# Loading the r and k tiles without their padding rows, seven loads in flight, and a newly drawn order

## The chip, the cores and the metric

The kernel runs on one core of a Trainium2 chip. The metric is the device time of one execution in microseconds; the median of several executions is compared.

## The reference

Two stages follow each other. The first is a linear attention with a decaying state, for 4 batches, 8 heads, 768 tokens and 48 dimensions a head:

```
cur   = (u * k_t) outer v_t
y_t   = r_t @ (state + cur)
state = w * state + k_t outer v_t
```

The second is a gated block on x, which is y with its heads laid side by side (384 columns):

```
h = relu(x @ w_in);  u, v = halves of h            (512 columns each)
v_n = (v - mean) / sqrt(var + 1e-6)
v_s = w_spatial @ v_n + b_spatial                  (over the 768 tokens)
out = (u * v_s) @ w_out
```

## The kernel before

**Chunks.** The 768 tokens of a batch are cut into 6 chunks of 128, 24 chunks for the 4 batches. For each chunk four transfers are issued in `load_chunk`: `rk` (r and k with the dimensions on the rows, for the scores), `rs` and `ks` (r and k with the tokens on the rows) and `rkv` (v). The `rk` tile has 128 rows of 4 KB: two heads share a tile, one on rows 0 to 63 and one on rows 64 to 127, and of each 64 rows 48 hold data. The other 16 are zeros, which the host writes and every load brings along. There are two buffers for `rk` tiles. `prep` multiplies the tile in place with powers of the decay (`tt`), for the first 13 chunks as two instructions that may go to POOL (GpSimd) or DVE (VectorE), then as one on DVE. Since the powers of the padding rows are 1, their zeros stay zeros. `scores` reads the tile on TensorE (PE), `apply` reads its r half (in the first eight chunks straight from the tile, later from a copy in tile `A`).

**The gated block.** `moe_v`, `moe_u`, `moe_sp` and `moe_out` follow once their chunks are there. Every float32 product is made of three matmuls of a high and a low part (`mm3`). The weights w_in and w_out arrive as 64-bit numbers and are split into high and low parts on DVE, ACT (ScalarE) and PE in the first part of the kernel (`convert_in`, `convert_out`), those of w_spatial by `split`.

**The order.** No engine's order is written by hand. The class `Plan` collects tasks with their costs on each engine, their buffers and what they depend on, and walks through them in simulated time, so that each engine's instructions come out in one order. All inputs go through the queue of SP (SyncE). The planner has a model of that queue: `landing` says when a load lands, from a delay to the first byte (`TO_BYTE`), a lower rate in the first microseconds (`SLOW`) and a rate after (`RATE`). `LANES` is the number of loads that may be in flight: every load waits, on the chip too, until the load six places before it has landed. `Fetch` models the fetching of PE's instructions and `Clock` TensorE's clock. Before the walk, `shake` goes through the list `SEEDS`; each seed stands for a small random change of some tasks' due times and of their leanings to one engine. With another list of seeds the whole order is another.

Of the kernel before, what the change touches and what calls it, by code (L numbers as in the profile page):

```python
# [8 lines left out]
F32 = mybir.dt.float32  # L9
# [3 lines left out]
ALU = mybir.AluOpType  # L13
AX = mybir.AxisListType

B, H, S, D = 4, 8, 768, 48
# [3 lines left out]
P = 128  # L20
C = 128
# [3 lines left out]
NP = H // 2  # L25
# [14 lines left out]
LEAN = 4.0  # L40
AHEAD = 0.3
ALONE = 1000.0
CALM, LATE = 80.0, dict(DVE=1.0, SP=1.0)
SEEDS = (786675, 590737, 650567, 473966, 410529, 555426, 907183, 123843, 647820, 960324, 828658, 912501, 134089,
         159232, 4393, 523669, 612611, 964576, 241432, 346394, 906374, 371707, 92393, 507276, 798277, 338735, 176835,
         444512, 896537, 239246, 993420, 861971, 866320, 990367, 131959, 191835, 802215, 648123, 562279, 390339,
         978361, 670519, 812235, 451845, 697243, 382570,)
BIAS = dict(DVE=3.0, ACT=3.5)
MOST_IN, MOST_OUT = 2, 1

# [3 lines left out]
CHAIN = dict(PE=0.0, DVE=0.115, ACT=0.11, POOL=0.0, SP=0.0)  # L54
SWITCH = {"bs": 0.095, "br": 0.095, "by": 0.095, "sb": 0.215, "sy": 0.11, "rb": 0.105, "yb": 0.105}
STAY = 1.0
LANES = 6
PORT = dict(DVE=(0.07, 0.0, 0.0), POOL=(0.15, 0.06, 0.02))


# [58 lines left out]
class Plan:  # L119
# [1 line left out]

    SLOW, PART = 210e3, (6.0, 42.0)
    RATE, TO_BYTE, BEHIND_BYTE = (395e3, 395e3, 262e3), (2.2, 2.9, 1.3), (0.5, 0.5, 0.4)

    def __init__(self, slots, wait):
        self.wait, self.sent = wait, []
# [45 lines left out]
    def shake(self):  # L174
        for seed in SEEDS:
            rnd = random.Random(seed)
            share, size = rnd.choice((0.01, 0.03, 0.1, 0.3)), rnd.choice((1.0, 3.0, 8.0))
            width, at = rnd.choice((3.0, 12.0, 50.0, 1000.0)), rnd.uniform(-10.0, 330.0)
            for t in self.tasks:
                if abs(t.due - at) < width and rnd.random() < share:  # L180
                    t.due += rnd.uniform(-size, size)
                    for w in t.ways:
                        w.lean += rnd.uniform(-size, size)
# [20 lines left out]
    def landing(self, line, at, nbytes):  # L204
        part = sum(at > x for x in self.PART)
        line = max(line, at + self.TO_BYTE[part])
        slow = min(nbytes / self.SLOW, max(0.0, 5.2 - line))
        line += slow + (nbytes - slow * self.SLOW) / self.RATE[part]
        return line, line + self.BEHIND_BYTE[part]

# [2 lines left out]
    def lane(self, at, landed):  # L213
        return max(at, landed[-LANES]) if len(landed) >= LANES else at

    def run(self):
# [8 lines left out]
        while ready:  # L225
# [71 lines left out]
            if way.nbytes:  # L297
                self.sent.append(made.ins)
                if len(self.sent) > LANES:
                    self.wait(made.ins, self.sent[-1 - LANES].name)  # L300
        assert all(t.end is not None for t in self.tasks)
# [3 lines left out]
def fused_kernel(ctx, tc, rkT, rkvE, rkvL, wT, uB, w_in, w_sp, b_sp, w_out, out):  # L305
# [9 lines left out]
    SLOTS = dict(rk=2, rs=2, ks=2, rkv=3, a=1, A=2, t=4, X=2, gt=4, u=8, vs=2, g=3, ob=2, pm=5, ps=1, xp=1, x=2, s=2, t1=1, dg=2, q=2)  # L315
    SLOTS |= {f"w{x}{n}": 1 for x in "ab" for n in range(NS)}
    const = ctx.enter_context(tc.tile_pool(name="const", bufs=1))
# [7 lines left out]
    plan = Plan(SLOTS, wait)  # L325
    T = {}

    def tile_of(key, shape, dtype=F32):
        key = key[:2]
        if key not in T:  # L330
            home = psum if key[0] in ("pm", "ps", "xp") else sbuf
            T[key] = home.tile(shape, dtype, name=key[0], tag=f"{key[0]}{plan.slot[key]}")
        return T[key]
# [6 lines left out]
    def dve(n, f, r, w, cost=None, two=False, due=None):  # L340
        plan.add([("DVE", n / 960 + 0.07 if cost is None else cost, f, two)], r, w).most = due
# [7 lines left out]
    def pair(n, f, r, w, ways="DVE POOL", lean=0.0):  # L349

        engine = dict(DVE=nc.vector, POOL=nc.gpsimd)
        cost = dict(DVE=n / 960 + 0.07, POOL=n / 480 + 0.17)
        plan.add([(e, cost[e], lambda e=e: engine[e].tensor_tensor(**f()), True, 0, lean if e == "DVE" else 0.0)  # L353
                  for e in ways.split()], r, w)
# [12 lines left out]
    def load(key, shape, dtype, src, nbytes, view=None, due=None):  # L367
        def f():
            t = tile_of(key, shape, dtype)
            return nc.sync.dma_start(out=view(t) if view else t, in_=src)  # L370
        plan.add([("SP", 0.45, f, False, nbytes)], (), [key], lag=0).most = due


    wt = const.tile([P, NP], F32, name="wt")
    ub = const.tile([P, DM], F32, name="ub")
    tt = const.tile([P, NP, C], F32, name="tt")
# [14 lines left out]
    def eye():  # L391
        return tile_of(EYE, [P, P])

    def neg(n=1):
        return tile_of(NEG, [P, 2, P], F32R)[:, n]
# [65 lines left out]
    TTP = ("pm", "tt")  # L461
    TN = [("c", "tn", 0), ("c", "tn", 1)]

    def load_chunk(m):
        b, c = divmod(m, NC)
        load(("rk", m), [P, 2, NP, C], F32, rkT[b, c], P * 2 * NP * C * 4)
        n, src = (ROW_E, rkvE[m]) if m < EC else (ROW, rkvL[m - EC])
        load(("rs", m), [P, DM], F32, src[:, 0:DM], P * DM * 4)
        load(("ks", m), [P, DM], F32, src[:, OK:OV], P * DM * 4)
        load(("rkv", m), [P, ROW - OV], F32, src[:, OV:n], P * (n - OV) * 4, lambda t: t[:, 0:n - OV])  # L470
# [116 lines left out]
    def prep(m):  # L587
        RK, RS, KS, DG, A = ("rk", m), ("rs", m), ("ks", m), ("dg", m), ("a", m)
        a = lambda: tile_of(A, [P, 2, 2, 2, HC])
        r_, k_, kn, rn = (RK + ("r",), RK + ("k",), KS + ("kn",), RS + ("rn",))  # L590
        rk = lambda: T[RK]
        TT = [("c", "t0"), ("c", "t1"), ("c", "t2")]
        if m < EARLY:
            for i, key in ((1, k_), (0, r_)):
                plan.add([("POOL", 1.24, lambda i=i: nc.gpsimd.tensor_tensor(
                    out=rk()[:, i], in0=rk()[:, i], in1=tt, op=ALU.mult), True),
                    ("DVE", 0.6, lambda i=i: nc.vector.tensor_tensor(
                        out=rk()[:, i], in0=rk()[:, i], in1=T[TTP].rearrange("p (n c) -> p n c", n=NP),
                        op=ALU.mult), False, 0, LEAN if i else -9.0)], [RK, TTP, *TT], [key])
        else:  # L600
            dve(1024, lambda: nc.vector.tensor_tensor(out=rk(), in0=rk(), in1=tt.unsqueeze(1).to_broadcast(  # L601
                [P, 2, NP, C]), op=ALU.mult), [RK, *TT], [r_, k_], cost=1.14, two=True)
        n_, k0 = (lambda: T[RS]), (lambda: T[KS])
        lean = ALONE if m < QUIET else LEAN
        pair(DM, lambda: dict(out=n_(), in0=n_(), in1=k0(), op=ALU.mult), [RS, KS], [rn], lean=lean)
        pair(DM, lambda: dict(out=n_(), in0=n_(), in1=ub, op=ALU.mult), [rn, ("c", "ub")], [rn], lean=lean)
        dve(DM - 8, lambda: nc.vector.tensor_reduce(out=tile_of(DG, [P, H]), in_=n_().rearrange("s (h d) -> s h d", h=H),
                                                axis=AX.X, op=ALU.add), [rn], [DG])
        pair(DM, lambda: dict(out=k0(), in0=k0(), in1=tn_f, op=ALU.mult), [KS, rn, *TN], [kn], lean=lean)
        pair(432, lambda: dict(  # L610
            out=a().rearrange("s b q z t -> s (b q z) t"), in0=diag.unsqueeze(1).to_broadcast([P, H, HC]),
            in1=T[DG].unsqueeze(2).to_broadcast([P, H, HC]), op=ALU.mult), [DG, ("c", "diag")], [A], lean=lean)
        if m >= EC:
            move(RK + ("r",), ("A", m), "r", [(64 * (1 - t), t, slice(2 * b, 2 * b + 2), 64 * (t ^ b))
                                              for b in range(2) for t in range(2)],
                 lambda p, h: rk()[h:h + 64, 0, p])

    def move(src, dst, part, places, source):

        for o, t, p, h in places:  # L620
            n = (p.stop - p.start) * C
            out = lambda o=o, t=t, p=p: tile_of(dst, [P, 2, NP, C])[o:o + 64, t, p]
            plan.add([("SP", 0.45, lambda out=out, p=p, h=h: nc.sync.dma_start(out=out(), in_=source(p, h)), False, 64 * n * 4),
                      ("ACT", (n + 250) / 1200, lambda out=out, p=p, h=h: nc.scalar.copy(out(), source(p, h))),  # L624
                      ("DVE", n / 1920 + 0.15, lambda out=out, p=p, h=h: nc.vector.tensor_copy(out=out(), in_=source(p, h)),  # L625
                       True, 0, LEAN)],
                     [src], [dst + ((part, t, p.start),)])
# [411 lines left out]
    for i in range(NM):  # L1039
        n = FIRST[i] if i < NC else len(steps) if i == NM - 1 else int(10 + (i - 5) * per / 6)  # L1040
# [20 lines left out]
    for b in range(B):  # L1061
        for c in range(NC):
            m = b * NC + c
# [93 lines left out]
```

## Time and profile before

| | |
|---|---|
| median of 3 runs | 326.91 us (326.5 to 327.86) |
| profiled execution | 327.6 us, of which the span of the profile is 325.9 us |
| TensorE (PE) busy | 309.7 us, 95% of the span |
| DVE, ACT, POOL busy | 245.4, 198.6, 250.9 us |
| mean granted TensorE clock | 0.995 |
| DMA | 49.14 MB, mean 151 GB/s |

The span runs from the first to the last instruction; the profiled execution has 1.7 us more around it. An engine's busy time counts the time in which at least one of its instructions ran. The granted clock is a share of TensorE's full speed. The DMA share is the mean busy share of the core's 16 DMA engines, and it can come out a little over 1.

### The profile page before, as it was taken

To read this page: it belongs to the slowest core of one execution; us is meant where nothing else is said; L and a number is where in the kernel's file an instruction comes from. 1 tells how busy PE (TensorE), PEld (TensorE's weight loads), DVE (VectorE), ACT (ScalarE), POOL (GpSimd) and SP (SyncE) were. 2 spreads that over 40 slices of the span, in tenths; PEclk is the share of its full clock that TensorE was granted. 3 is DMA by queue.
4 is the path that set the end of the run, shared out by engine and by line. 5 is a ranking of instruction groups with operands and counts; after the bars stand their busy time and mean duration, and the time that the engine had idled before them with its cause. 6 is when DMAs were issued, how large, how long until landed. Compare 5 with 4: busy or idle time off the path is not lost.

```text
span 325.9 us, 10933 instructions
## 1 busy us (share of the span) xinstructions
PE 309.7 (95%) x4574; PEld 283.3 (87%) x4574; DVE 245.4 (75%) x465; ACT 198.6 (61%) x492; POOL 250.9 (77%) x235
## 2 busy tenths in 40 slices
PE   2787999999999999999999999999999999999995
PEld 1466788999999888998979998999988989999995
DVE  6899986799962899858999996489998431727830
ACT  4346984847643887767759477686576663433422
POOL 3878999999988999899999875688999440358700
PEclk9997999999999999999999999999999999999999
DMA  6999768685255836154346245264140010010013
GB/s 229 377 393 382 257 219 278 217 295 181 91 172 185 270 100 235 32 178 141 106 166 203 51 177 171 81 205 139 51 147 5 25 50 2 0 51 24 0 42 105
DMA packets 21233, 49.14 MB, mean 151 GB/s; under 512 B 2496, under 2 KB 12096, under 8 KB 21184
## 3 DMA queue, kind: packets, MB, share of 16 engines
q1 hardware_dynamic: 21040, 48.34, 43.2%
q8 instruction: 36, 0.59, 0.8%
q14 instruction: 13, 0.11, 0.1%
q10 hardware_dynamic: 144, 0.10, 0.1%
HBM read 43.58 MB, written 4.72 MB: 148 GB/s over the span
## 4 chain that ended last, share of the span: by engine, by line
PE 68%; DVE 10%; POOL 8%; DMA 7%; ACT 3%; issue 2%; SPq 0%; POOLq 0%; ACTq 0%; DVEq 0%
PE pm L762 20%; PE pm L764 19%; PE pm L763 19%; PE xp L719 5%; DMA rs<-rkvE 4%; PE ps L638 3%; POOL rs L353 2%; DMA rk<-rkT 2%; DMA wb<-w_sp 2%; PE ps L657 1%; DVE rk L601 1%; POOL wb L353 1%; DVE A L625 1%; POOL t L353 1%; DVE a L353 1%
## 5 line engine op out<-in xcount | busy, mean ns | idle before, releaser
L762 PE MATMUL pm<-wa,t 128*128 128x384 f32 x120 | 41.3, 344 | 0.0
L763 PE MATMUL pm<-wa,t 128*128 128x384 f32 x120 | 40.5, 337 | 0.0
L764 PE MATMUL pm<-wa,t 128*128 128x384 f32 x120 | 40.4, 336 | 0.0
L353 POOL TENSOR_TENSOR t<-vs,t 128x384 fp32r<-128x384 f32 x26 | 32.6, 1269 | 1.4 <-ACT t L358 1.4
L762 PE MATMUL pm<-x,wi_h 128*128 128x384 f32 x93 | 32.0, 344 | 0.0
L764 PE MATMUL pm<-x,wi_l 128*128 128x384 f32 x93 | 31.2, 336 | 0.0
L763 PE MATMUL pm<-x,wi_h 128*128 128x384 f32 x93 | 31.2, 336 | 0.0
L624 ACT COPY A<-rk 64x256 f32<-64x256 f32 x54 | 21.8, 404 | 15.1 <-PE xp L719 5.3
L353 POOL TENSOR_TENSOR rs<-rs,ks 128x384 f32<-128x384 f32 x21 | 26.8, 1276 | 4.4 <-DMA ks<-rkvL 2.9
L762 PE MATMUL pm<-wi_h,x 128*128 128x512 f32 x69 | 28.5, 413 | 0.3 <-DVE g L933 0.3
L762 PE MATMUL pm<-wo_h,gt 128*128 128x384 f32 x84 | 28.6, 340 | 0.0
L764 PE MATMUL pm<-wo_h,gt 128*128 128x384 f32 x84 | 28.3, 336 | 0.0
L763 PE MATMUL pm<-wo_l,gt 128*128 128x384 f32 x84 | 28.3, 336 | 0.0
L764 PE MATMUL pm<-wi_h,x 128*128 128x512 f32 x69 | 27.7, 401 | 0.0
L763 PE MATMUL pm<-wi_l,x 128*128 128x512 f32 x69 | 27.5, 399 | 0.0
L353 POOL TENSOR_TENSOR ks<-ks,tn 128x384 f32<-128x384 f32 x23 | 25.1, 1092 | 0.0
L353 POOL TENSOR_TENSOR rs<-rs,ub 128x384 f32<-128x384 f32 x22 | 23.4, 1062 | 1.3
L353 POOL TENSOR_TENSOR X<-vs,X 128x384 f32<-128x384 f32 x9 | 10.6, 1175 | 17.6 <-ACT vs L844 17.2
L933 DVE TENSOR_TENSOR g<-pm,bb 128x384 f32<-128x384 f32 x32 | 17.5, 549 | 8.6 <-PE pm L764 8.2
L353 POOL TENSOR_TENSOR a<-diag,dg 128x512 f32<-128x512 f32 x16 | 17.2, 1077 | 8.5 <-ACT A L624 7.6
L353 POOL TENSOR_TENSOR gt<-u,gt 128x384 fp32r<-128x384 f32 x20 | 22.6, 1142 | 1.3 <-ACT gt L358 1.3
L762 PEld LDWEIGHTS pm<-wa,t 128*128 128x128 f32 x120 | 22.6, 188 | 1.1 <-DVE g L933 0.6
(182 smaller groups left out, 960.4 us busy)
## 6 DMA issues: line engine op xcount, KB each, us to landing
rk<-rkT SPq DMA_DIRECT2D x24, 512.0 KB, 5.6
rkv<-rkvL SPq DMA_DIRECT2D x16, 512.0 KB, 3.8
out<-ob SPq DMA_DIRECT2D x23, 192.0 KB, 2.0
wa<-w_in SPq DMA_DIRECT2D x6, 512.0 KB, 5.5
rkv<-rkvE SPq DMA_DIRECT2D x8, 384.0 KB, 5.9
rs<-rkvL SPq DMA_DIRECT2D x16, 192.0 KB, 2.7
ks<-rkvL SPq DMA_DIRECT2D x16, 192.0 KB, 5.2
wb<-w_sp SPq DMA_DIRECT2D x6, 384.0 KB, 5.4
```

The lines of the kernel that those rows point to most:

```text
L353: plan.add([(e, cost[e], lambda e=e: engine[e].tensor_tensor(**f()), True, 0, lean if e == "DVE" else 0.0) for e in ways.split()], r, w)
L601: dve(1024, lambda: nc.vector.tensor_tensor(out=rk(), in0=rk(), in1=tt.unsqueeze(1).to_broadcast([P, 2, NP, C]), op=ALU.mult), [RK, *TT], ...
L624: ("ACT", (n + 250) / 1200, lambda out=out, p=p, h=h: nc.scalar.copy(out(), source(p, h))),
L625: ("DVE", n / 1920 + 0.15, lambda out=out, p=p, h=h: nc.vector.tensor_copy(out=out(), in_=source(p, h)), True, 0, LEAN)],
L638: nc.tensor.matmul(ps[64 * hf:64 * hf + 64, b, o:o + HC], rk[hd, 1, p, s0:s0 + 64], rk[hd, 0, p, t0:t0 + 64], start=True, stop=True, skip_ ...
L657: nc.tensor.matmul(ps[64 * j:64 * j + D, b, o:o + D], kn[hs, kc:kc + D], ve[hs, h, z, p, slice(0, D) if m < EC else slice(16 * h, 16 * h + ...
L719: nc.tensor.matmul(xp[32 * p:32 * p + 32, o:o + HC], lhsT, rhs, start=p not in began, stop=True, skip_group_check=True, tile_position=(0, ...
L762: nc.tensor.matmul(o, lh, rh, start=first, stop=False, skip_group_check=free)
L763: nc.tensor.matmul(o, lh, rl, start=False, stop=False, skip_group_check=free)
L764: nc.tensor.matmul(o, ll, rh, start=False, stop=last, skip_group_check=free)
L933: dve(TH, lambda: nc.vector.tensor_tensor(out=g(K), in0=T[PM][:, 0:TH], in1=other(), op=ALU.add), [PM, ("c", "bb"), *r], [K])
```

## The change

Four things are changed. The two `rk` buffers become fixed tiles, and only the first load into each (chunks 0 and 1) brings all 128 rows; from chunk 2 on two loads of 48 rows each, to rows 0 to 47 and 64 to 111, leave the zeros of the padding rows where they are. The multiplication in `prep` then depends on both. `LANES` goes from 6 to 7, and each half counts as a load. The planner's model of the first loads has other constants. The list of seeds is a new one, of 189 numbers in place of 46; according to the change's title it was chosen by 24 replays of each plan with late loads and jitter. That choice was made outside the kernel, which holds the list alone.

```diff
-SEEDS = (786675, 590737, 650567, 473966, 410529, 555426, 907183, 123843, 647820, 960324, 828658, 912501, 134089,
...
+SEEDS = (510017, 789016, 349449, 4415, 22282, 162314, 413315, 599960, 460165, 632294, 15888, 576524, 887186, 388971,
...
-LANES = 6
+LANES = 7
...
-    SLOW, PART = 210e3, (6.0, 42.0)
-    RATE, TO_BYTE, BEHIND_BYTE = (395e3, 395e3, 262e3), (2.2, 2.9, 1.3), (0.5, 0.5, 0.4)
+    SLOW, PART = 240e3, (6.0, 42.0)
+    RATE, TO_BYTE, BEHIND_BYTE = (395e3, 395e3, 262e3), (0.95, 2.9, 1.3), (0.5, 0.5, 0.4)
...
-        slow = min(nbytes / self.SLOW, max(0.0, 5.2 - line))
+        slow = min(nbytes / self.SLOW, max(0.0, 6.0 - line))
...
     def tile_of(key, shape, dtype=F32):
         key = key[:2]
+        if key[0] == "rk":
+            return T.setdefault(key, pairs[plan.slot[key]])
...
+    pairs = [const.tile([P, 2, NP, C], F32, name=f"rk{n}") for n in range(SLOTS["rk"])]
...
     def load_chunk(m):
         b, c = divmod(m, NC)
-        load(("rk", m), [P, 2, NP, C], F32, rkT[b, c], P * 2 * NP * C * 4)
+        if m < SLOTS["rk"]:
+            load(("rk", m), [P, 2, NP, C], F32, rkT[b, c], P * 2 * NP * C * 4)
+        else:
+            for h in range(2):
+                rows = lambda t, h=h: t[64 * h:64 * h + D]
+                load(("rk", m, h), [P, 2, NP, C], F32, rows(rkT[b, c]), D * 2 * NP * C * 4, rows)
...
-                        op=ALU.mult), False, 0, LEAN if i else -9.0)], [RK, TTP, *TT], [key])
+                        op=ALU.mult), False, 0, LEAN if i else -9.0)], [RK, RK + (0,), RK + (1,), TTP, *TT], [key])
         else:
             dve(1024, lambda: nc.vector.tensor_tensor(out=rk(), in0=rk(), in1=tt.unsqueeze(1).to_broadcast(
-                [P, 2, NP, C]), op=ALU.mult), [RK, *TT], [r_, k_], cost=1.14, two=True)
+                [P, 2, NP, C]), op=ALU.mult), [RK, RK + (0,), RK + (1,), *TT], [r_, k_], cost=1.14, two=True)
```

## Rows read from the trace of the kernel before

**Rows 1.** The page: span and busy time of each engine.
```profile
span 325.9 us, 10933 instructions
PE 309.7 (95%) x4574; PEld 283.3 (87%) x4574; DVE 245.4 (75%) x465; ACT 198.6 (61%) x492; POOL 250.9 (77%) x235
```

**Rows 2.** Windows: stretch, length; busy PE, PEld, DVE, ACT, POOL; clock, DMA share, GB/s.
```profile
5.00:34.00 29.00, 22.28 (x542) 15.72 (x542) 26.54 (x50) 15.17 (x38) 21.68 (x21) 0.94 1.02 378
5.00:42.00 37.00, 29.94 (x700) 22.30 (x704) 34.44 (x70) 22.35 (x57) 29.48 (x29) 0.95 0.94 346
...
42.00:322.00 280.00, 278.83 (x3870) 260.46 (x3870) 207.71 (x388) 173.64 (x430) 218.41 (x192) 1.00 0.38 126
```

**Rows 3.** Chain of waits, 12 to 33 us: start, duration, what.
```profile
12.61 6.73 DMA rs<-rkvE
...
25.00 5.56 DMA wb<-w_sp
...
31.18 1.01 POOL wa L353
32.19 0.78 issue
```

**Rows 4.** Windows, the load pipe in the start-up and around 67 us.
```profile
12.60:30.60 18.00, 15.46 (x356) 10.84 (x355) 17.10 (x34) 9.85 (x25) 15.46 (x16) 0.91 1.02 386
...
66.00:68.00 2.00, 2.00 (x14) 2.00 (x13) 2.00 (x5) 1.33 (x5) 2.00 (x2) 1.00 1.01 392
68.25:69.00 0.75, 0.75 (x7) 0.75 (x6) 0.69 (x2) 0.71 (x2) 0.75 (x1) 1.00 0.93 335
```

**Rows 5.** Timeline of POOL, 33 to 36 us.
```profile
33.01 1.27 POOL L595 TENSOR_TENSOR rk<-rk,tt 128x512 f32<-128x512 f32 x1 [0.82 <-DMA rk<-rkT]
34.24 1.05 POOL L353 TENSOR_TENSOR a<-diag,dg 128x512 f32<-128x512 f32 x1
```

**Rows 6.** Timeline of SP's queue, the rk issues from 17 to 27 us.
```profile
17.57 0.33 SPq L370 DMA_DIRECT2D rk<-rkT  x1
...
26.01 0.33 SPq L370 DMA_DIRECT2D rk<-rkT  x1
```

**Rows 7.** Timeline of PE, 25 to 35 us, its three waits.
```profile
25.34 0.30 PE L719 MATMUL xp<-a,rkv 128*32 128x64 f32 x2 [1.59 <-issue]
26.36 0.73 PE L638 MATMUL ps<-rk 64*64 64x64 f32 x32 [0.72 <-issue]
...
34.34 0.69 PE L638 MATMUL ps<-rk 64*64 64x64 f32 x32 [0.76 <-POOL rk L595]
```

**Rows 8.** Windows of 2 us behind the stall.
```profile
26.00:28.00 2.00, 1.64 (x65) 1.58 (x66) 2.00 (x5) 1.61 (x5) 1.92 (x3) 0.72 1.00 367
28.00:30.00 2.00, 2.00 (x6) 1.52 (x6) 1.97 (x5) 1.97 (x6) 2.00 (x3) 0.50 1.01 362
30.00:32.00 2.00, 2.00 (x57) 1.48 (x55) 2.00 (x5) 1.41 (x4) 1.59 (x2) 0.92 1.03 405
```

**Rows 9.** DMA view: queues from 21 to 26 us, rk issues from 5 to 34.
```profile
q1 hardware_dynamic: 819, 1.97, 102.2%
q8 instruction: 1, 0.02, 1.1%
...
rk<-rkT SPq DMA_DIRECT2D x4, 512.0 KB, 6.4
```

**Rows 10.** Line 623: the two moves of r into 64 rows.
```profile
L623 SPq DMA_DIRECT2D A<-rk x2: 462/498/534, 66.6 to 67.4; - x2
...
DMA to landing us min/median/max: 3.7/3.9/4.2
```

**Rows 11.** Waits of SP's queue, 0 to 45 us: total, times, longest.
```profile
SPq L370 <- DMA wa<-w_in: 6.1, 6, 1.7
SPq L370 <- DMA rk<-rkT: 3.9, 4, 1.3
```

**Rows 12.** Waits of PE, 100 to 322 us.
```profile
PE pm L764 <- POOL t L353: 0.8, 1, 0.8
```

More of the change, by code (lines that the diff above doesn't have):

```diff
@@ L43 @@
 CALM, LATE = 80.0, dict(DVE=1.0, SP=1.0)
-SEEDS = (786675, 590737, 650567, 473966, 410529, 555426, 907183, 123843, 647820, 960324, 828658, 912501, 134089,
-         159232, 4393, 523669, 612611, 964576, 241432, 346394, 906374, 371707, 92393, 507276, 798277, 338735, 176835,
-         444512, 896537, 239246, 993420, 861971, 866320, 990367, 131959, 191835, 802215, 648123, 562279, 390339,
-         978361, 670519, 812235, 451845, 697243, 382570,)
+SEEDS = (510017, 789016, 349449, 4415, 22282, 162314, 413315, 599960, 460165, 632294, 15888, 576524, 887186, 388971,
[14 rows of a table added]
 BIAS = dict(DVE=3.0, ACT=3.5)
```

14 rows, old and new, of the table SEEDS are left out of this document.

## The prediction

> **What bounds the kernel now.** I read the busy times first: TensorE (PE) is busy for 309.7 us of the span of 325.9 us [rows 1]. 16.2 us of idle time are left, so the question is where they lie. The windows say it [rows 2]: from 42 to 322 us PE is busy for 278.83 of 280.00 us, 1.17 us idle; from 5 to 42 us it is busy for 29.94 of 37.00, 7.06 us idle. The rest, 8.0 us, lies ahead of 5 us and behind 322 us, before the first load has landed and while the last rows go out. The change orders no more and no less for PE to compute, so a gain can come from three places: the start-up up to 42 us, the 1.17 us in the middle, and the half microsecond here and there that another order of PE's blocks costs or saves.
>
> What sets the start-up is the chain of waits [rows 3]: from 12.61 to 30.57 us it holds nothing but three transfers (the first takes 6.73, the last 5.56 us), each issued when an earlier one had landed. The loads are one full pipe there: the DMA share is 1.02 at 386 GB/s from 12.6 to 30.6 us [rows 4], and 1.02 over all of 5 to 34 us [rows 2]. The chain then goes through the split of a w_sp tile, POOL's part of it last, to a piece of 0.78 us for which it names no work, and from there to POOL's multiplication of the r and k tile of the fourth chunk at 33.01 us [rows 5] and to that chunk's scores on PE at 34.34 [rows 7]. POOL's own timeline says what the 0.78 us were: POOL sat idle for 0.82 us until the rk load landed [rows 5]. That load was issued at 26.01 us [rows 6], and PE idles 0.76 us for what it feeds [rows 7]. Behind it PE is saturated. So the start-up is paid in bytes of load, as long as VectorE (DVE) keeps up: it is busy 34.44 of the 37.00 us from 5 to 42 us, so some 2.5 us at most can be won before it is the bound.
>
> A second loss has nothing to do with bytes. In the apply block of the third chunk PE stops after 46 of 48 matmuls and goes on 1.59 us later, and then 0.72 us more pass before the next scores; both waits are put down to "issue", that is, to nothing that the profile shows [rows 7]. [...] Idle and clock together: 1.59 + 0.72 + 1.62 = 3.93 us. The one instruction transfer (queue q8) from 21 to 26 us runs there beside load queue q1 at 102.2% [rows 9]; that the stall is that fetch is my reading, not a row's.
>
> **The change, part by part.**
>
> *Smaller rk loads.* From the third chunk on a load of 128 rows (512 KB, 4 KB a row) becomes two of 48 rows, 384 KB in all. At 386 GB/s the whole took 524,288 B / 386 GB/s = 1.36 us of the pipe; two halves take 1.02 us if they move at the same rate, 0.34 us less. Two such loads lie ahead of the wait at 33.01 us (issued at 17.57 and 26.01 us [rows 6]), so the fourth chunk's rk lands 0.68 us sooner. PE's wait there is 0.76 us, so the 0.68 us can be taken whole. Later rk loads are hidden under a PE that has no idle time; the traffic is 22 x 0.13 MB = 2.9 MB less, and from 42 us on the DMA share is only 0.38 [rows 2], so that is worth nothing.
>
> Do 48 rows move at the full rate? Before has no such load. The nearest rows are the two moves of r into 64 rows of tile A, issued around 67 us, 64 KB each, landed 3.7 and 4.2 us later [rows 10]. In the stretch in which they can have moved, 68.25 to 69.00 us, the pipe did 335 GB/s at a share of 0.93, which is 360 at full share, against 392 / 1.01 = 388 from 66 to 68 us [rows 4]. That is 7% less and not half, with smaller rows and other traffic mixed in. So the gain lies between 0.68 us and, were the halves to move at half the rate (2.04 us a pair), a loss of 0.68 us each, 1.36 us for two. I take the gain, since the nearest rows are near the full rate.
>
> [...]
>
> *Twice as many rk issues.* 22 more on SP's queue at about 0.33 us each [rows 6], 7 us in all, two of them ahead of 33 us. They are hidden: SP waits 6.1 + 3.9 us in the first 45 us for landings of wa and rk alone [rows 11]. Were that cover gone, the two would cost 0.7 us.
>
> *Seven loads in flight.* A full pipe is not filled further, so by itself this is 0. What is queued ahead of a new load changes: a chunk's four loads were 512 + 192 + 192 + 384 KB, six of the mean are 1,920 KB; five are now 4 x 192 + 384, seven of the mean 1,613 KB, a sixth less. Issue to landing, 6.4 us for rk from 5 to 34 us [rows 9], should fall toward 5.4 us. The multiplication now waits for both halves; what queues behind it on POOL is the chunk's diagonal product [rows 5], which needs neither, so a half that comes late delays that as before.
>
> *New constants of the planner and new seeds.* These cost no instruction; they change the order in which every queue issues. Work per engine stays, but for pieces that may go to another engine. In the middle they have 1.17 us to win, and I see no row that prices what they could lose there; 0 taken, 1.2 won to 1.6 lost kept. (The largest single wait there is 0.8 us [rows 12], and twice that is my bound on a loss.) In the start-up they can win up to the 3.93 us of the stall and its slow clock, or leave all of it, or pay it twice. The stall stands at a place in PE's stream and at a time when the load queue is full; another order of blocks changes both, and a stall that falls where PE waits for data anyway costs nothing. I take a third of it, 1.2 us; the ends are 0 and 3.93 won and 3.93 lost.
>
> **Sum.** Against the profiled execution: 327.6 us (325.9 of span and 1.7 around it) - 0.68 - 1.2 = 325.7 us. That execution lies 0.7 above the median of the runs, 326.91, which the prediction is for: 326.91 - 1.88 = 325.0 us. A measurement of this kernel can tell about 0.5%, 1.6 us, from no change: under 325.3 is faster, over 328.5 slower.
>
> **Rivals.**
> 1. *Another order, the same time.* The bytes are saved, but the stall stays, and DVE, 93% busy in the start-up, takes up what the loads give: 326.91 - 0.68 to 326.91, about 326.5. For it speaks that the middle is already 99.6% busy; against it that POOL and PE did wait for the rk load itself.
> 2. *Halves at half rate.* The change doesn't do what it says: each pair is longer in the pipe than the whole tile was. At +1.36 us it is 328.3 with nothing won by the order, 327.1 with the 1.2 us. For it speaks that before has no load of fewer than 128 rows of data, so that nothing in its rows excludes it; against it the 360 GB/s beside the 64-row moves. [...] The DMA share in the start-up would stay at 1.0 while the rate falls under 386 GB/s.
> 3. *A second stall, the other side.* In PE's first 42 us the new order puts one more break like that of 23.8 us into a stretch where PE has work, with the clock's fall behind it: 326.91 - 0.68 + 3.93 = 330.2. It decides from 0.68 + 1.6 = 2.3 us of idle and clock on. For it speaks that PE's stream in the start-up is that of 542 matmuls in 29 us [rows 2], with one such break already; against it that nothing in the change adds PE instructions.
>
> **How the numbers follow.** The forecast, fewer bytes and part of the stall, has 0.45 (its own range 322.3 to 325.9, from the whole stall won to a tenth of it); rival 1 has 0.25, rival 2 0.15, rival 3 0.15. Faster by over 0.5%: 0.41 of the forecast and 0.05 of rivals 1 and 2 with a calmer middle, 0.46. Slower: 0.14 of rival 3, 0.02 of rival 2, 0.16. Between: 0.38. The range leaves out the upper part of rival 3 and the lowest end of the forecast: 322.6 to 328.4 us.
>
> **What would show it.** Right: the rk halves issued from about 17 us on land in under 6 us; the 5-to-34 us rate stays near 380 GB/s; the wait of POOL for the fourth chunk's rk is gone or PE's saturation begins before 34 us; PE's idle time from 5 to 42 us falls from 7.06 to about 5.5 us; the windows without full clock shrink. Wrong: a rate well under 380 GB/s at full share (rival 2); an "issue" wait of PE over 1.5 us between 10 and 42 us followed by a clock of 0.5 as before or twice (rivals 1 and 3); idle time of PE from 42 to 322 us over 3 us, which none of my terms holds.

## The result and the profile after

The changed kernel takes 331.27 us (330.56 to 331.52, 4 runs) beside 326.94 us of before: a ratio of 1.0125, interval 1.0098 to 1.0152. Run again beside the experiments on another occasion it gave 1.0080 (1.0051 to 1.0110). It is slower by about 1%, or 2.6 to 4.3 us. The forecast was 1.9 us faster, and the time lies outside the range. Where a median and a ratio below don't fit together, the ratio counts: it compares undisturbed runs only. "Before" was a little slower on the two chips of the experiments (medians of 328.1 to 328.7 us), so kernels are set against each other by their ratios.

The page and the windows of the changed kernel, columns as in [rows 1, 2]:

```profile
span 329.3 us, 11014 instructions
PE 312.0 (95%) x4574; PEld 283.9 (86%) x4574; DVE 239.3 (73%) x461; ACT 199.9 (61%) x491; POOL 248.5 (75%) x234
...
q1 hardware_dynamic: 21168, 45.99, 47.4%
```

```profile
5.00:34.00 29.00, 23.06 (x450) 15.67 (x454) 25.63 (x48) 14.05 (x34) 18.41 (x18) 0.88 1.02 345
5.00:42.00 37.00, 30.60 (x685) 21.59 (x686) 30.98 (x58) 20.73 (x52) 23.72 (x23) 0.91 1.00 319
...
22.00:24.00 2.00, 1.83 (x59) 1.10 (x62) 2.00 (x5) 1.11 (x3) 0.77 (x1) 1.00 1.07 191
...
26.00:28.00 2.00, 0.95 (x38) 0.70 (x41) 1.50 (x3) 1.07 (x3) 1.74 (x3) 0.83 1.06 395
28.00:30.00 2.00, 2.00 (x35) 1.69 (x36) 2.00 (x5) 0.99 (x3) 1.92 (x3) 0.50 0.94 303
30.00:32.00 2.00, 2.00 (x6) 1.59 (x5) 1.97 (x6) 1.95 (x5) 2.00 (x3) 0.50 1.02 305
32.00:34.00 2.00, 2.00 (x39) 1.27 (x41) 1.73 (x3) 0.89 (x4) 0.83 (x1) 0.50 1.03 227
34.00:36.00 2.00, 1.90 (x105) 1.68 (x95) 0.32 (x1) 1.06 (x4) 0.79 (x1) 0.97 1.02 235
...
42.00:322.00 280.00, 276.71 (x3862) 258.04 (x3861) 204.99 (x395) 175.37 (x432) 221.73 (x196) 1.00 0.42 119
```

Three things stand there. First, the load pipe is still full in the start-up (share 1.02), but it moves 345 GB/s from 5 to 34 us where it moved 378 [rows 2], and 191 GB/s at a share of 1.07 from 22 to 24 us. Fewer bytes are in the pipe, and the pipe is slower; over the whole kernel the load queue moved 2.4 MB less (2.9 MB less of rk, 0.5 MB more of moves that the new order gives to this queue) and took a larger share of the 16 engines (47.4% beside 43.2%). A busy share alone would have hidden this. Second, DVE, the engine that I had feared as the next bound, is less busy in the start-up: 30.98 us where it was 34.44. Its longest waits from 5 to 42 us are 2.0 us for ACT and 1.7 us in two parts for rk tiles. Third, the clock stays at 0.50 from 28 to 34 us in this profile, longer than before [rows 8].

The chain of waits of the changed kernel (start, duration, what) goes through the changed loads, where it went through `rs` and w_sp before [rows 3]:

```profile
17.37 7.95 DMA rk<-rkT
...
27.64 8.36 DMA rk<-rkT
...
36.02 5.96 DMA rk<-rkT
...
42.07 0.69 DVE rk L616
42.76 0.61 DVE wi_l L525
```

And this is the place of [rows 7] in PE's timeline. The prediction calls the broken block the third chunk's apply; it is the second chunk's, since only two blocks of scores stand ahead of it (13.83 and 20.14 us). The scores behind it are the third chunk's:

```profile
26.09 0.27 PE L738 MATMUL xp<-a,rkv 128*32 128x64 f32 x2 [1.28 <-issue]
...
27.86 1.13 PE L657 MATMUL ps<-rk 64*64 64x64 f32 x32 [0.96 <-POOL rk L614]
```

The break after 46 of 48 matmuls is there again, 1.28 us in place of 1.59, and behind it PE waits for the rk tile. The middle is hurt as well. One such wait, followed back through the chain, DVE's timeline and PE's timeline:

```profile
146.84 6.27 DMA rk<-rkT
```

```profile
153.20 2.08 DVE L620 TENSOR_TENSOR rk<-rk,tt 128x1024 f32<-128x1024 f32 x1 [3.75 <-DMA rk<-rkT]
```

```profile
161.75 0.41 PE L781 MATMUL pm<-wa,t 128*128 128x384 f32 x1 [1.66 <-ACT t L371]
```

DVE sits idle for 3.75 us until a pair has landed, works off what has piled up, and 8.5 us later PE waits 1.66 us for a split that came late. No line of PE names rk there; only the chain does. In all, DVE waits 14.6 us for rk from 42 to 322 us (total, times, longest), where it waited 5.1 us before:

```profile
DVE rk L620 <- DMA rk<-rkT: 9.5, 4, 3.8
DVE rk L616 <- DMA rk<-rkT: 5.1, 3, 3.8
```

**The account against before**, by the spans, 329.3 - 325.9 = 3.4 us: PE's idle time from 5 to 42 us is 6.40 us for 7.06, -0.66. The slow clock costs 0.5 x 6.00 from 28 to 34 us and 0.2 at its edges, 3.2 us for 1.62, +1.6. The middle idles 3.29 us for 1.17, +2.1. Together 3.0 of the 3.4 us.

The split of the start-up into idle time and slow clock is not the same in every execution. The second profile of this kernel (from its second set of runs, a span of 328.7 us) has the same break, and the clock never falls:

```profile
5.00:42.00 37.00, 28.44 (x687) 19.86 (x687) 32.30 (x60) 21.48 (x55) 24.77 (x24) 1.00 0.99 322
42.00:322.00 280.00, 277.10 (x3861) 258.35 (x3862) 204.79 (x394) 175.03 (x430) 221.33 (x196) 1.00 0.42 119
```

```profile
26.33 0.27 PE L738 MATMUL xp<-a,rkv 128*32 128x64 f32 x2 [1.59 <-issue]
...
37.61 0.69 PE L657 MATMUL ps<-rk 64*64 64x64 f32 x32 [1.95 <-DVE ps L723]
```

PE idles 8.56 us there in place of 6.40, and the span is 0.6 us shorter, not 3.2: most of what the slow clock took in the first profile is idle time in the second. So idle time and clock are taken together: the start-up loses 9.6 and 8.6 us in the two profiles, where before lost 8.7; the middle idles 3.3 and 2.9 us, where before idled 1.2. The loss in the middle is in both profiles. Against the second one these two make 1.6 of the 2.8 us; the rest is not found.

### The profile page after: what moved, and what is told of

Its sections match the earlier page's. It is cut to its first block, busy times and chain, and to the rows that moved or that the text cites. A ratio compares the mean times of both kernels' runs of the same rounds, so it can differ in the third digit from the quotient of the medians.

```text
span 329.3 us, 11014 instructions
## 1 busy us (share of the span) xinstructions
PE 312.0 (95%) x4574; PEld 283.9 (86%) x4574; DVE 239.3 (73%) x461; ACT 199.9 (61%) x491; POOL 248.5 (75%) x234
## 3 DMA queue, kind: packets, MB, share of 16 engines
q1 hardware_dynamic: 21168, 45.99, 47.4%
## 4 chain that ended last, share of the span: by engine, by line
PE 72%; DMA 18%; DVE 4%; issue 2%; SPq 2%; ACT 1%; POOL 1%; DVEq 0%; ACTq 0%
PE pm L781 21%; PE pm L783 20%; PE pm L782 20%; DMA rk<-rkT 15%; PE xp L738 6%; PE ps L657 3%; DMA wa<-w_in 2%; DMA ks<-rkvL 2%; PE ps L676 2%; SPq L383 2%; DVE rk L620 0%; DVE g L952 0%; DVE rk L616 0%; DVE rs L366 0%; POOL rk L614 0%
## 5 line engine op out<-in xcount | busy, mean ns | idle before, releaser
L366 POOL TENSOR_TENSOR a<-diag,dg 128x512 f32<-128x512 f32 x22 | 24.4, 1109 | 10.8 <-ACT A L643 6.3
L366 POOL TENSOR_TENSOR rs<-rs,ks 128x384 f32<-128x384 f32 x17 | 21.5, 1262 | 13.7 <-DMA ks<-rkvL 5.4
L366 POOL TENSOR_TENSOR t<-vs,t 128x384 fp32r<-128x384 f32 x25 | 29.7, 1205 | 2.1 <-ACT t L371 2.0
L643 ACT COPY A<-rk 64x256 f32<-64x256 f32 x50 | 20.2, 405 | 11.7 <-PE xp L738 7.6
L620 DVE TENSOR_TENSOR rk<-rk,tt 128x1024 f32<-128x1024 f32 x11 | 18.9, 1721 | 9.5 <-DMA rk<-rkT 9.5
L366 POOL TENSOR_TENSOR u<-g,u 128x384 f32<-128x384 f32 x19 | 20.9, 1098 | 5.8 <-DVE g L952 4.3
L366 POOL TENSOR_TENSOR ks<-ks,tn 128x384 f32<-128x384 f32 x21 | 23.3, 1110 | 0.0
L366 POOL TENSOR_TENSOR t<-X,t 128x384 fp32r<-128x384 f32 x18 | 21.8, 1216 | 1.3 <-ACT t L371 1.2
```

## The experiments

### The rate of loads by the rows that they cover

The computation is left out; the kernel moves tiles of r and k only, seven loads in flight. Its stages:

```diff
+    def halves(t, s, u):
+        for r in (0, 64):
+            put(t[r:r + D], s[r:r + D])
...
+    for stage in (whole, halves, low, columns, across, joined, whole):
+        for n in range(2 * N):
+            stage(tiles[n % N], rkT[n // NC, n % NC], tiles[(n + N // 2) % N])
```

> This kernel leaves out the whole computation and only moves r and k tiles, seven loads in flight, in stages: 16 loads of 128 rows; 32 of 48 rows, in turn to rows 0 to 47 and 64 to 111; 32 of 48 rows, all to rows 0 to 47; 32 of 128 rows and half the columns; 32 of 48 rows, all to rows 40 to 87; 16 of 112 rows; 16 of 128 rows. Every row piece is 4 KB but in the stage of half columns (2 KB). Theory A, the rows that a load covers set its rate (the 191 GB/s at a DMA share of 1.07 that the changed kernel shows from 22 to 24 us): about 390 GB/s for 128 rows and for half columns, about 200 for both stages of 48 rows in one half of the tile, clearly over 200 for the same 48 rows laid across the middle (40 to 87), about 390 for 112 rows. Theory B, the number of rows or the small size of the load sets it: rows 40 to 87 are as slow as rows 0 to 47. Theory C, the rate fell in the changed kernel for another reason (its order, its mix): all stages lie between 350 and 400 GB/s.

Windows within the seven stages in that order (stretch, length, busy POOL, clock, DMA share, GB/s):

```profile
8.00:16.00 8.00, 0.00 (x0) 1.00 1.02 414
27.00:48.00 21.00, 0.00 (x0) 1.00 1.05 233
57.00:88.00 31.00, 0.00 (x0) 1.00 1.05 158
104.00:112.00 8.00, 0.00 (x0) 1.00 1.03 384
118.00:134.00 16.00, 0.00 (x0) 1.00 1.04 294
142.00:160.00 18.00, 0.00 (x0) 1.00 1.04 276
166.00:180.00 14.00, 0.00 (x0) 1.00 1.03 410
```

Whole tiles: 414 and 410 GB/s. Pairs of 48 rows in turn: 233. 48 rows always in the lower half: 158. The same 48 rows laid across the middle of the tile: 294. So B and C fall: equally many rows of equal size move nearly twice as fast at another place. Theory A holds for the place, but it missed sizes: 158 and 233 GB/s where it said about 200 for both, and 276 GB/s for 112 rows where it said 390. Half columns reach 384 GB/s in the window shown; from 92 to 108 us, a stretch that begins ahead of it, the pipe was not full (303 GB/s at a share of 0.89). The rows read and the rows written shift together in these stages, so which of the two sides sets the rate is not told apart. The time of a whole tile is 0.524 MB / 412 = 1.27 us, that of a pair 0.393 / 233 = 1.69 us. The pair has three quarters of the bytes and takes a third longer.

In the kernel the pairs stand between loads of 128 rows, so a second kernel of this kind put a whole tile behind each:

```diff
...
+    for stage in (between(halves), between(columns), between(whole), most):
```

> This kernel leaves out the whole computation and only moves r and k tiles, seven loads in flight, in stages of 16 steps: a pair of 48-row loads (rows 0 to 47, then 64 to 111) and a whole tile; two loads of half the columns and a whole tile; two whole tiles; then 16 loads of 96 rows, rows 0 to 95. From the rates of the first stages alone (409 GB/s for whole tiles, 233 for pairs): if a pair keeps its price between whole tiles, 0.39 MB / 233 + 0.52 MB / 409 = 1.69 + 1.28 = 2.97 us a step, 309 GB/s. If the whole tiles beside it hide it, since then not all of the loads in flight go to the same half: near 1.02 + 1.28 = 2.3 us a step, about 400 GB/s. Half columns and whole tiles: about 400 GB/s. 96 rows, if the rows in one half set the time: 0.39 MB in the time of a whole tile, 1.28 us, about 307 GB/s; if the bytes alone do: about 400.

```profile
10.00:50.00 40.00, 0.00 (x0) 1.00 1.04 237
66.00:96.00 30.00, 0.00 (x0) 1.00 1.04 398
106.00:132.00 26.00, 0.00 (x0) 1.00 1.03 409
148.00:158.00 10.00, 0.00 (x0) 1.00 1.04 250
```

Both expectations for the first stage were too kind: 0.918 MB a step at 237 GB/s are 3.87 us. Less 1.28 us for the whole tile (at 409), a pair costs 2.59 us there, about what two loads of 48 rows cost at the 158 GB/s of the lower half (2.49 us): the whole tiles beside it hide none of it. Half columns between whole tiles keep 398 GB/s. And 96 rows in one load move at 250 GB/s, 1.57 us: longer than the 128 rows that they are part of.

### The loads alone, in the new order

Every engine's instructions stay in the changed kernel's order; only the cut of the rk loads is another, so that each covers all 128 rows.

```diff
-                rows = lambda t, h=h: t[64 * h:64 * h + D]
-                load(("rk", m, h), [P, 2, NP, C], F32, rows(rkT[b, c]), D * 2 * NP * C * 4, rows)
+                cols = lambda t, h=h: t[:, h]
+                load(("rk", m, h), [P, 2, NP, C], F32, cols(rkT[b, c]), D * 2 * NP * C * 4, cols)
```

> The changed kernel with every engine's order of instructions kept, but the two rk loads of a chunk take all 128 rows and half the columns each (256 KB, 512 KB in all) in place of 48 rows and all columns (192 KB, 384 KB in all). Theory A, loads of 48 rows move at about half the rate: though a third more bytes are loaded, most of the 4.3 us lost comes back, 327 to 328.5 us; the rate at full DMA share in the start-up is back near 390 GB/s. Theory B, the new order itself is the loss: 331 us or more, since more bytes are loaded than that order was made for. Theory C, seven loads in flight are the loss: 331 us, too.

Measured: 323.57 us, a ratio of 0.9868 (0.9812 to 0.9924). That is not only better than the changed kernel but better than before by 1.3%, more than theory A gave, and B and C fall: with these loads the new order and seven in flight are a gain, and loads of 48 rows more than eat it up. Its windows:

```profile
5.00:34.00 29.00, 23.15 (x550) 16.26 (x551) 27.67 (x53) 16.55 (x42) 20.74 (x21) 1.00 1.03 395
5.00:42.00 37.00, 31.08 (x763) 22.68 (x764) 34.99 (x72) 24.17 (x62) 28.66 (x28) 1.00 0.95 358
...
42.00:318.00 276.00, 275.99 (x3805) 258.59 (x3803) 200.85 (x382) 172.99 (x424) 216.47 (x192) 1.00 0.40 128
```

395 GB/s where the changed kernel had 345; the clock never falls; PE idles 0.01 us from 42 to 318 us. Of the 8.0 us between the two spans (329.3 and 321.3) 3.7 us are idle time and slow clock in the start-up (9.6 less 5.92) and 3.3 us idle time in the middle. The break of PE in the second chunk's apply is still there, but shorter (0.77 us), and PE's clock stays up:

```profile
24.54 0.27 PE L738 MATMUL xp<-a,rkv 128*32 128x64 f32 x2 [0.77 <-issue]
...
26.14 0.69 PE L657 MATMUL ps<-rk 64*64 64x64 f32 x32 [0.66 <-POOL rk L614]
...
34.50 0.69 PE L657 MATMUL ps<-rk 64*64 64x64 f32 x32
```

A second time, on another chip:

> The kernel with two rk loads of half the columns each (all 128 rows, 512 KB), in the order of the changed kernel, seven loads in flight; a second time, beside the next two on one chip. Ratio to before 0.983 to 0.991 as the first time (0.9868); a ratio over 0.995 would mean that the first was chance.

0.9873 (0.9821 to 0.9924). This is the version that beats both kernels. Between the two profiles on the later occasions (spans of 328.7 and 323.1 us, full clock in both start-ups) 2.7 of the 5.6 us are idle time in the start-up (8.56 less 5.89) and 1.9 us idle time in the middle (2.90 less 0.96):

```profile
5.00:42.00 37.00, 31.11 (x754) 22.36 (x758) 34.13 (x71) 23.53 (x61) 28.04 (x28) 1.00 0.94 352
...
42.00:318.00 276.00, 275.04 (x3820) 257.63 (x3810) 205.88 (x384) 173.65 (x424) 216.91 (x192) 1.00 0.40 128
```

### The loads alone, in the old order

```diff
...
+            if key[0] == "rk" and key[1] >= SLOTS["rk"]:
+                return [nc.sync.dma_start(out=t[r:r + D], in_=src[r:r + D]) for r in (0, 64)]
             return nc.sync.dma_start(out=view(t) if view else t, in_=src)
...
```

A pair counts as one of the six loads in flight here.

> The kernel before with every engine's order kept and six loads in flight, but from the third chunk on an rk load is issued as two of 48 rows, one right behind the other, the first waiting for both parts of what it waited for. Theory A (half the rate): two pairs ahead of the fourth chunk's scores, each about 0.7 us longer in the pipe than the whole tile, so 1.4 us later there, and more where rk loads of later chunks come late: 328.3 to 330 us. Theory B (the new order is the loss): 326.3 us, the 0.7 us of saved bytes. Theory C (seven in flight): the same as B.

1.0121 (1.0062 to 1.0181), 4.0 us of 328.74: theory A, and more than its 1.4 to 3.1 us. The start-up moves 340 GB/s, and PE idles 3.82 us in the middle, where before idled 1.17:

```profile
5.00:34.00 29.00, 22.06 (x454) 15.34 (x458) 25.72 (x48) 13.79 (x33) 20.71 (x20) 0.88 1.01 340
...
42.00:322.00 280.00, 276.18 (x3852) 256.97 (x3851) 209.98 (x398) 173.34 (x431) 219.54 (x194) 1.00 0.41 115
```

Of PE's waits in the start-up the one for POOL's rk tiles is as before (4.0 us in all, 4.1 before); the break has grown from 1.59 to 2.8 us (total, times, longest):

```profile
PE ps L645 <- POOL rk L602: 4.0, 2, 3.3
PE xp L726 <- issue: 2.8, 1, 2.8
```

The halves cost as much in the old order as the whole change does, with the order of instructions and the number in flight unchanged.

### Six or seven loads in flight

Three kernels differ in this number alone from one with the same order and the same loads; one of them ran twice.

```diff
-                if len(self.sent) > LANES:
-                    self.wait(made.ins, self.sent[-1 - LANES].name)
+                if len(self.sent) > 6:
+                    self.wait(made.ins, self.sent[-1 - 6].name)
```

> The changed kernel with every engine's order kept, but six loads in flight in place of seven on the chip. Theory A (half the rate): the pipe is full either way, so 331 us within 0.7. Theory B (the order): the same. Theory C, seven in flight delay the loads that are needed first: faster by 1 us or more.

The changed kernel with six: 1.0215 (1.0142 to 1.0287), slower than with seven by about 1%. No theory had said so; C is the furthest off.

> The kernel before with every engine's order kept, but seven loads in flight in place of six on the chip. Theory L (a seventh load helps by itself, since loads that the order wants early are issued earlier): 1 to 3 us faster than before. Theory F (the pipe is full with six in the start-up, DMA share 1.02, so a seventh adds nothing): within 0.7 us of before.

Before with seven: 0.9978 (0.9954 to 1.0002), 0.7 us: theory F, within what can be told from no change. The changed kernel ran beside it:

> The changed kernel once more, on the chip of the next three runs, so that they can be set against it as well as against the kernel before: a ratio of 1.010 to 1.015 to before is expected by every theory.

1.0080, a little under the range expected.

> The kernel with two rk loads of half the columns each, in the order of the changed kernel, but with six loads in flight on the chip. The same kernel with seven took 323.57 us beside 328.74 of before. Theory L: 2 us or more slower than that, a ratio to before of 0.993 or more. Theory F: the ratio stays near 0.987, and the gain is the order's alone.

> The same kernel with six loads in flight, beside it on the same chip. Theory L (a seventh load in flight is part of the gain): 1.5 to 2 us slower than with seven. Theory F (the pipe is full either way): within 0.7 us of it.

Half columns with six: 0.9913 (0.9887 to 0.9939), and 0.9963 (0.9925 to 1.0001) beside 0.9873 with seven on the same chip. So the seventh place is worth 0.4 to 0.9% in the new order, and F holds in the old one. The first of the two is weak: its interval overlaps that of seven (0.9812 to 0.9924), and it is short of theory L's sign, 0.993. In the old order seven adds nothing to a full pipe, as the prediction said; the new order was drawn with seven and loses where the chip holds to six. By which loads it loses I didn't trace; that it is the order's fit to the number is argued from these ratios alone.

### The whole tile in one load, and fewer bytes at the full rate

```diff
...
-                load(("rk", m, h), [P, 2, NP, C], F32, rows(rkT[b, c]), D * 2 * NP * C * 4, rows)
+                load(("rk", m, h), [P, 2, NP, C], F32, rkT[b, c], D * 2 * NP * C * 4, skip=h == 1)
```

> The changed kernel with every engine's order kept, but the first of the two rk loads of a chunk brings the whole tile of 128 rows (512 KB) and the second isn't issued. Bytes as before, one issue less, and seven loads in flight reach further ahead. If only the rate of the 48-row loads made the changed kernel slow: as fast as the kernel with half columns, a ratio of 0.983 to 0.990. If cutting the load in two helped there by itself (the first part may start sooner, 22 more places in flight): slower than that by 1 us or more.

0.9966 (0.9926 to 1.0007), with single times from 324.69 to 331.79 us: slower than half columns by about 1%, as if the cut in two helped, but the times scatter too much for a cause. So the rate alone does not make the whole difference between the changed kernel and half columns. Whole tiles against halves of 48 rows, both in the new order with seven in flight, are 1.1 to 1.6% (1.0080 and 1.0125 less 0.9966), near the 1.2% of the old order; the further 1% came with the cut in two columns. And with whole tiles the new order and seven in flight gain 0.3%, which can't be told from nothing.

In the last kernel each half-column load takes three of its four pairs of heads and leaves out the fourth:

```diff
-                cols = lambda t, h=h: t[:, h]
+                cols = lambda t, h=h: t[:, h, m // 2 % 2:m // 2 % 2 + 3]
```

> The kernel with half columns, but each of the two loads takes 384 of the 512 columns of all 128 rows (three of the four head pairs, in turn the first or the last three), so 384 KB a chunk as in the change, at what should be the full rate; a quarter of r and k is then stale, and the output wrong. This prices the bytes alone, the 0.68 us of the prediction. Theory A (bytes in the start-up set when TensorE is fed): 0.4 to 0.9 us faster than the kernel with half columns. Rival (VectorE, not the loads, bounds the start-up there, or the wait for rk is gone already): within 0.3 us of it.

0.9917 (0.9866 to 0.9968), fastest run 323.80 us beside 323.82 of half columns with all bytes. No gain from a quarter fewer bytes is to be seen. PE idles 5.45 us from 5 to 42 us in its profile, where half columns idle 5.92 and 5.89; but the times scatter up to 330.4 us, with a median of 329.21, so half a microsecond is neither shown nor excluded.

## Why the prediction was wrong

**The failed step is the rate of the smaller loads.** "Do 48 rows move at the full rate? ... I take the gain, since the nearest rows are near the full rate." They move at 233 GB/s among themselves and cost 2.59 us a pair among whole tiles, where the prediction had 1.02 us and, as its bad end, 2.04. So both the value and the bound were too good. This was rival 2, to which I gave 0.15; its sign that I named, a share of 1.0 at a falling rate, is what the windows show.

The nearest rows had been read too short. I took 68.25 to 69.00 us for the two moves into 64 rows [rows 4]; they landed 3.7 and 4.2 us after issues at 66.6 and 67.4 us [rows 10], so about 71 us. The windows of before right behind:

```profile
69.00:69.50 0.50, 0.50 (x4) 0.50 (x4) 0.47 (x2) 0.00 (x0) 0.50 (x2) 1.00 0.87 269
69.50:70.00 0.50, 0.50 (x19) 0.25 (x21) 0.50 (x2) 0.00 (x0) 0.50 (x1) 1.00 0.90 283
70.00:70.50 0.50, 0.50 (x52) 0.50 (x43) 0.49 (x2) 0.43 (x1) 0.50 (x2) 1.00 0.82 293
```

That is 309 to 357 GB/s at full share, where 388 was normal. Besides, 0.13 MB in a stretch full of other loads can't show a rate at all.

Why the place of the rows sets the rate is not shown. As measured, a load of 48 rows takes 1.24 us in the lower half (0.197 MB at 158 GB/s), hardly less than the 1.27 us of all 128, and 0.67 us on rows 40 to 87 (294 GB/s). Sending every second load to the other half raises the rate by 47% with nothing but pairs in flight (233 for 158 GB/s); among whole tiles the runs show no gain (2.59 us for a pair, 2.49 us for two loads to the lower half).

**Later rk loads are not hidden.** "Later rk loads are hidden under a PE that has no idle time", and a DMA share of 0.38, made me give them no price. The share is a mean; a late pair held DVE for 3.75 us and, by way of a split, PE for 1.66 us. The middle's idle time was to be within 1.2 us won and 1.6 lost; it lost 2.1 us in one profile and 1.7 in the other.

**The bytes, -0.68 us.** At the full rate they show no gain that can be told (0.9917 beside 0.9873). Part of the reason can be read: with half columns in the new order the fourth chunk's scores start on PE at 34.50 us without a wait, so there is no wait for that tile left to shorten. The term is not shown; PE's idle time in one profile gives it some 0.45 us.

**The order, -1.2 us,** has the right sign with half columns, and its size stays open. It is then 1.3% (4.3 us) together with the seventh place and the cut in two, with whole tiles 0.3% (1.1 us, between 2.4 and nothing). Between the profiles of before and of half columns (325.9 and 321.3 us) the start-up idles 1.14 us less (7.06 less 5.92), the middle 1.16 us less, and the slow clock's 1.62 us are gone. The break of PE stayed where it was, 0.77 us for 1.59; that another order would hide it was not borne out. The third of the bound that I took was a guess.

**The price of the slow clock, 1.62 us,** was too high. The prediction counted it in full among the 3.93 us to be won. No run shows it as time lost: it is an estimate, PE's busy time in the three windows of [rows 8] times what the clock lacks of 1.00 there (1.64 x 0.28 + 2.00 x 0.50 + 2.00 x 0.08). The runs showed in its place a difference of 0.6 us at most between the averages at full clock and below. The changed kernel's five runs on the later occasion lie between 330.30 us (mean clock 1.000) and 330.78 (0.995), the one at 0.990 at 330.63; eight runs of before with a clock of 0.998 or more average 328.2 us, fifteen with less 328.1, and on the other chip seven average 327.5 and fifteen 328.1. In this start-up a slow clock takes the place of idle time more than it adds time.

**Seven in flight, 0,** was right in the old order, and wrong as a term of its own in the new one, where six cost 0.4 to 0.9%. The shorter time to landing that I worked out from the bytes in flight came out the other way: 8.9 us from issue to landing for the halves from 5 to 34 us, where the whole tile took 6.4 [rows 9]:

```profile
rk<-rkT SPq DMA_DIRECT2D x4, 192.0 KB, 8.9
```

**The second stall (rival 3)** didn't come. In one profile the slow clock behind the first break took 3.2 us for 1.62, with a wait of 0.96 us for rk between; in the other the break was 1.59 us and the clock stayed up. What decides between the two is not shown.

What stays open: what a quarter fewer bytes is worth in this start-up, why 96 and 112 rows (250 and 276 GB/s) are slower than 128 (409 to 414 GB/s), whether the rows read or the rows written set the rate, what the cut in two columns adds, and which loads profit from the seventh place.

## What to carry to other kernels

Count the time of a load, not its bytes: leaving out rows of a tile can make its transfer longer, and here 128 rows with padding (1.28 us) beat two loads of 48 rows (2.59 us among whole tiles) and one of 96 (1.57 us) without. Read rate and busy share of the DMA together, over the whole stretch up to the landing, and price a new shape of transfer by a run of its own before it goes into a kernel. When several edits are made at once, keep the order of instructions and undo one: here the same order was 1.3% faster than before with half columns and about 1% slower with loads of 48 rows. And take a second profile before pricing a slow clock.

## What was new about the hardware

Two loads of 48 rows between loads of 128 rows cost 2.59 us where one load of all 128 rows costs 1.28 us, at DMA shares of 1.04 and 1.03. A single load of 96 rows (1.57 us at 250 GB/s) is slower than one of 128. The same 48 rows move at 158 GB/s on rows 0 to 47 and at 294 on rows 40 to 87.
